# Splitting the first weights of two experts whole instead of in halves, inside a fused attention and two mixture-of-experts layers

## The chip, the cores and the metric

The kernel runs on one core of a Trainium2 chip. The metric is the time of one execution on the device in microseconds (us), the median of several runs; less is better. Engines are named as the profile names them: PE is TensorE, DVE is VectorE, ACT is ScalarE, POOL is GpSimd, SP is the engine that issues most DMAs.

## What is computed

Three layers follow each other, all on float32 inputs: a linear attention with a root-mean-square norm, a mixture of experts in which every token goes through all four experts, and a soft mixture with eight experts of four slots. The second layer is the long one:

```python
N, D, E, F = (2304, 512, 4, 1024)
p = domain_probs / (domain_probs.sum(-1, keepdims=True) + 1e-09)
out = np.zeros((N, D), dtype=np.float32)
for e in range(E):
    h = np.maximum(x @ w1[e], 0.0)
    out += p[:, e:e + 1] * (h @ w2[e])
```

The output must agree with a float32 reference, so a float16 product alone would be too coarse.

## The kernel before

**Products.** Each float32 operand is scaled and split into two float16 pieces, a high one (the rounded value) and a low one (what is left). A product is then three float16 matmuls: high by high, high by low, low by high. On top of this, each large product is a 2 by 2 block product done with seven block products instead of eight (Winograd's form). So each expert's w1, which arrives as four raw pages of 128 by 1024 (blocks 0 to 3), is turned into seven operands, B11, B21, B22 and T1 to T4, of which the T are differences of raw blocks (T1 = block 1 - block 0, T2 = block 3 - T1, T3 = block 3 - block 1, T4 = block 2 - T2). SBUF is managed as 47 pages of 128 by 1024 floats.

**Splitting.** The function split (lines 612 to 619) makes one operand's pieces: the high piece by an ACT instruction (line 615), the low piece by a DVE instruction (line 617). Each takes 512 columns of an operand in this kernel (the method put, line 666), apart from expert 0, whose w1 is split 1024 columns at a time with the methods hi and lo (lines 670 and 673) at the start of the program. The differences are made by make (line 643, a DVE instruction of 1024 columns at line 652). The same split is used for w2 (line 712) and for differences of w2 blocks (prep_t2, line 722, whose subtractions are line 735).

**Main list.** The 18 tiles of 128 tokens are taken in chunks: chunks 0 and 1 first (four tiles each), then the rest. The program builds one list of 542 steps, each about 1.3 us of PE work. A step of mm1 is one half of one of the seven block products with w1 (12 matmuls of 256 columns, line 926); a step of mm2 multiplies with w2 (line 989, the plain form, 6 matmuls of 512 columns into one bank for each tile of tokens, read out by DVE at line 1001), and a step of mm2_fast does a block product of the second layer (12 matmuls of 256 columns, line 1029). For experts 1 and 2 the order of the steps is mm1 of chunk 0, mm1 of chunk 1, mm2 of chunk 0 (16 steps), mm2_fast of chunk 1 (14 steps). For expert 1 these are steps 60 to 73, 74 to 87, 88 to 103 and 104 to 117; for expert 2 the same from 118 to 175.

**mm2_fast and its banks.** The seven block products come in the order 1, 7, 6, 4, 5, 2, 3 (ORDER3), each as two steps (two pairs of tiles, j = 0 and 1). Products 1, 6, 5, 3 accumulate in one bank ("x"), 7 and 4 in a second, 2 in a third. After each product DVE reads both halves of the bank and adds them into the output (line 1051, two instructions). Product 6 writes into the bank of product 1, so it waits until DVE has read product 1 out of it. Product 1 takes the bank that the second token tile of mm2 has left, product 7 that of the third.

**Evictions of mm1 for chunk 1.** They run in fast_h: DVE adds product 2 (line 864), 7 (line 868) and 3 (line 872) to what ACT has copied, ACT and DVE split the sums (lines 834, 836 and 841, 845), and a queue of further work (todo: lines 879, 883, 849) is taken off one item a step.

**Background work.** Preparations run beside the main list as chains: a chain is a list of small steps that is spread over a range of main steps by a credit, with a weight per main step that depends on the phase.

```python
credit += wt[0] * (len(steps) - credit) / max(sum(wt), 1e-3)
n = min(int(credit + 1e-6), max(1, -(-len(steps) // len(wt))))
```

Engines execute what is issued to them in program order, so where a chain's step falls decides what DVE and ACT do before what. The weights of expert e (2 or 3) are prepared by one chain over the steps of expert e - 1: prep_w1 and then prep_w2. prep_w1 is 10 steps that find the scale (the four w_size are ACT instructions, line 538), then 15 steps that split 14 halves; step n of these issues the low piece of half n - 1 and the high piece of half n. The weights of the phases are 0.5, 0.1, 0.5 and 1.0, so few steps fall into mm1 of chunk 1. At the same time a second chain, prep_t2 of expert e - 1, runs.

Of the kernel before, what the change touches and what calls it, by code (L numbers as in the profile page):

```python
# [33 lines left out]
B11, B21, B22, T1, T2, T3, T4 = range(7)  # L34
# [13 lines left out]
def attn_moe_softmoe_kernel(ctx: ExitStack, tc: tile.TileContext, qT, k, v, g, dp, w1, w2, phi, m1, m2a, m2b, out):  # L48
# [482 lines left out]
    def w_size(e, nm, b):  # L531

        m = wmx.get((e, nm))
        if m is None:
            m = wmx[e, nm] = small.tile([128, 4], F32, tag=f"mx{nm}", name=f"mx_{nm}_{e}")
        src = need((nm, 0, e, b)).ap
        junk = work.tile([128, 1024], BF16, tag="junk", name=f"junk{e}_{b}")
        nc.scalar.activation(junk, src, AF.Square if nm == "w1" else AF.Abs, accum_out=m[:, b:b + 1])  # L538
# [24 lines left out]
    def scale_steps(e, nm):  # L563

        return [lambda: w_scale_a(e, nm), lambda: None, lambda: None, lambda: None, lambda: pe(lambda: w_spread(e, nm)),
                lambda: w_scale_b(e, nm)]
# [45 lines left out]
    def split(dst, src, s, part):  # L612

        if part == 0:
            nc.scalar.activation(dst[:, 0], src, AF.Copy, scale=s)  # L615
        else:
            nc.vector.scalar_tensor_tensor(  # L617
                out=dst[:, 1], in0=src, scalar=s, in1=dst[:, 0], op0=ALU.mult, op1=ALU.subtract
            )

    class PrepW1:
# [44 lines left out]
        def put(self, op, i, part):  # L666
            dst = self.page(op).rearrange("p (s k n) -> p s k n", s=2, k=2)
            split(dst[:, :, i], self.src(op).f32(2)[:, i], wpw[self.k[1], "w1"][1], part)
# [11 lines left out]
    def prep_w1(g_, e, eng):  # L680
        w = PrepW1(g_, e, eng)
        st = []
        if g_ == 0:
            st += [lambda b=b: w_size(e, "w1", b) for b in range(4)]
            st += scale_steps(e, "w1")

        then = {
            B11: lambda: w.make(T2),
            T2: lambda: w.make(T4),
            T1: lambda: w.t1.release(),  # L690
            T4: lambda: (w.drop(0), w.drop(2)),
            T3: lambda: w.drop(1),
            B22: lambda: w.drop(3),
        }
        seq = [(op, i) for op in (B11, B21, T2, T1, T3, B22, T4) for i in range(2)]

        def step(n):
            if n == 0:
                w.make(T1)
            if n == 2:  # L700
                w.make(T3)
            if n > 0:
                op, i = seq[n - 1]
                w.put(op, i, 1)
                if i == 1 and op in then:
                    then[op]()
            if n < len(seq):
                w.put(*seq[n], 0)

        return st + [lambda n=n: step(n) for n in range(len(seq) + 1)]  # L710

    def w2_split(e, b, key, i, part):
        pgs = w2p.setdefault((0 if key == b or e > 0 else 1, e), {})
# [262 lines left out]
    def mm2(wk, c, t, u, kk, first, bank=ps_o):  # L976
        if t // 2 not in acc:
            acc[t // 2] = Page(first)
        o = (t - CH[c][0]) * 128
        if u == 0 and kk == 0:  # L980
            yps[t] = bank(f"y{wk[0]}_{wk[1]}_{t}")
        ps = yps[t]
        h = h_view(c, u, kk)
        w = w2_page(wk, 2 * kk + u).f16().rearrange("p (s f n) -> p s f n", s=2, f=2)
        for fp in range(2):
            hh, hl = (h[:, s, fp, o:o + 128] for s in range(2))
            wh, wl = (w[:, s, fp] for s in range(2))
            for i, (a, b) in enumerate(((hh, wh), (hh, wl), (hl, wh))):
                nc.tensor.matmul(  # L989
                    ps, a, b, start=(u + kk + fp + i == 0), stop=(u == 1 and kk == 1 and fp == 1 and i == 2)  # L990
                )
        work_off(1)
        if u == 0 or kk == 0:
            return
        del yps[t]
        x = acc_f32(t)
        pc = pcs[wk[1]][:, t:t + 1]
        if first:
            nc.vector.tensor_scalar(out=x, in0=ps, scalar1=pc, scalar2=None, op0=ALU.mult)
        else:  # L1000
            nc.vector.scalar_tensor_tensor(out=x, in0=ps, scalar=pc, in1=x, op0=ALU.mult, op1=ALU.add)
# [284 lines left out]
    for gi, cs in enumerate(GR):  # L1286
        for ei, e in enumerate(EXP[gi]):
# [5 lines left out]
            seq = [(i, c) for c in cs for i in (1, 2)]  # L1293
            if gi == 0 and e in SOON:
                seq = [(i, c) for i in (1, 2) for c in cs]
            if gi == 1:
                seq = LASTSEQ if ei == E - 1 else FASTSEQ
            runs.append((e, [(gi, i, c) for i, c in seq]))
    for e, seq in runs:
        if True:  # L1300
            for n, (gi, which, c) in enumerate(seq):
# [12 lines left out]
                if which == 1:  # L1314
                    if not turns:
                        own, other = ps_x, ps_o
                    st = [lambda wk=wk, c=c, u=u, P=P, fast=fast, bank=own: mm1(wk, c, u, P, fast, bank)
                          for P in ORDER for u in range(2)]
# [8 lines left out]
                elif fast:  # L1327
                    st = [lambda wk=wk, c=c, P=P, j=j, bank=own, ei=ei, apart=other if last and done else None:
                          mm2_fast(wk, c, P, j, bank, ei == 0, apart)
                          for P in ORDER3 for j in range(len(ch) // 2)]  # L1330
# [3 lines left out]
                else:  # L1334

                    tu = [(ch[0], 0), (ch[1], 0), (ch[0], 1), (ch[1], 1)] + [(t, u) for t in ch[2:] for u in range(2)]
                    st = [
                        lambda wk=wk, c=c, t=t, u=u, kk=kk, ei=ei, b=(own, other, other, own)[t % 4] if soon else ps_o:
                        mm2(wk, c, t, u, kk, ei == 0, b)
                        for t, u in tu for kk in range(2)  # L1340
                    ]
# [63 lines left out]
    for e in range(1, E):  # L1405
        chain(m["mm2", 0, 0, 0] + 12 if e == 1 else m["mm1", 0, e - 1, 0], m["end", 0, e - 1, 1] - 1,
              prep_w1(0, e, V) + prep_w2(0, e), 12 if e == 1 else 6,
              W1 if e == 1 else by_phase(e - 1, 0.5, 0.1, 0.5, 1.0))
# [60 lines left out]
    with tc.manual_schedule():  # L1469
# [13 lines left out]
        w = PrepW1(0, 0, nc.vector)  # L1483
# [392 lines left out]
```

## Time and profile before

| | |
|---|---|
| median of 3 runs | 812.72 us (812.07 to 816.3) |
| profiled execution, its own time | 812.28 us |
| its span, first to last instruction | 810.5 us |
| PE busy | 794.8 us, 98% |
| DVE busy | 579.3 us, 71% |
| ACT busy | 404.4 us, 50% |
| DMA | 126.03 MB, mean 155 GB/s |

All parts below come from the one profiled execution. Busy times of PE come from matmuls that overlap each other, and their ends are modelled, so a busy PE can still lose a little; where it waits, the timeline shows a gap with the instruction that ended it. [...]

### The profile page before, as it was taken

The numbers are of one execution on the slowest core, as the hardware profiler recorded it, in microseconds if no ns is written. First come the engines' busy times: TensorE is split into PE (matmuls) and PEld (weight loads), VectorE is DVE, ScalarE is ACT, GpSimd is POOL, SyncE is SP. The second block draws the span as 40 slices with busy tenths as digits, with TensorE's granted clock in tenths as the row PEclk, the third lists the DMA queues.
The fourth block names the chain that finished last, engine by engine and source line by source line (L and its number), as shares of the span: only waits on it lengthen the run. The fifth ranks groups of instructions, "written<-read, shape, count | busy, mean of one in ns | idle before, by whom it ended". The sixth has DMA issues, their size and how long they took to land.

```text
span 810.5 us, 17979 instructions
## 1 busy us (share of the span) xinstructions
PE 794.8 (98%) x7630; PEld 651.2 (80%) x7630; DVE 579.3 (71%) x1145; ACT 404.4 (50%) x791; POOL 5.9 (1%) x14
## 2 busy tenths in 40 slices
PE   8999999999999999999999999999999999999996
PEld 8876768668857867888988888998889889887544
DVE  6997968986998467789779547874578548676403
ACT  5876766566656244684656446231544137322203
POOL 0000000000000000000000000000000000000000
PEclk9999999999999999999999999999999999999998
DMA  9961532376417700200015750045004132669897
GB/s 359 404 256 46 192 153 79 130 260 235 155 62 261 251 1 10 71 2 1 1 53 186 283 183 1 19 165 206 4 1 169 66 131 79 242 214 339 311 398 239
DMA packets 40753, 126.03 MB, mean 155 GB/s; under 512 B 4066, under 2 KB 11106, under 8 KB 40674
## 3 DMA queue, kind: packets, MB, share of 16 engines
q1 hardware_dynamic: 40016, 124.57, 42.3%
q8 instruction: 59, 0.97, 0.5%
q10 hardware_dynamic: 658, 0.33, 0.1%
q14 instruction: 20, 0.16, 0.1%
HBM read 96.57 MB, written 28.31 MB: 154 GB/s over the span
## 4 chain that ended last, share of the span: by engine, by line
PE 90%; DVE 7%; ACT 1%; issue 1%; DVEq 0%; POOL 0%; POOLq 0%; ACTq 0%
PE p L926 38%; PE m L1029 26%; PE y L989 13%; PE s L1725 2%; PE so L1755 2%; PE o L340 2%; PE keep L265 2%; PE kv L285 1%; DVE pages L617 1%; PE x2T L1068 1%; PE xT L405 1%; PE lg L1097 1%; DVE pages L1051 1%; DVE pages L845 1%; PE f L1788 1%
## 5 line engine op out<-in xcount | busy, mean ns | idle before, releaser
L926 PE MATMUL p<-pages 128*128 128x256 f16 (+1 forms) x3360 | 339.0, 262 | 0.5 <-ACT cT L1233 0.5
L926 PEld LDWEIGHTS <-pages 128*128 128x128 f16 x3360 | 299.8, 98 | 33.3 <-issue 2.0
L1029 PE MATMUL m<-pages 128*128 128x256 f16 x2184 | 244.7, 273 | 2.8 <-DVE pages L1051 1.6
L1029 PEld LDWEIGHTS <-pages 128*128 128x128 f16 x2184 | 213.0, 98 | 29.8 <-issue 3.7
L1051 DVE SCALAR_TENSOR_TENSOR pages<-m,pc,pages 128x256 f32<-128x256 f32 x162 | 72.3, 480 | 59.3 <-PE m L1029 58.7
L989 PE MATMUL y<-pages 128*128 128x512 f16 x480 | 106.1, 379 | 0.3 <-DVE pages L943 0.3
L989 PEld LDWEIGHTS <-pages 128*128 128x128 f16 x480 | 46.9, 98 | 54.1 <-DVE pages L943 0.8
L617 DVE SCALAR_TENSOR_TENSOR pages<-pages,s_w 128x512 f16<-128x512 f32 (+1 forms) x113 | 84.7, 780 | 3.3 <-ACT pages L615 3.0
L836 ACT CAST pages<-t 128x512 f16<-128x512 f32 (+1 forms) x90 | 49.9, 562 | 72.6 <-DVE t L879 36.7
L615 ACT ACTIVATE pages<-pages,s_w 128x512 f16<-128x512 f32 (+1 forms) x113 | 79.1, 742 | 12.9 <-DVE s_w L591 9.7
L845 DVE TENSOR_TENSOR pages<-t,pages 128x512 f16<-128x512 f32 (+1 forms) x90 | 54.2, 614 | 3.4 <-ACT pages L836 2.3
L834 ACT ACTIVATE pages<-pages 128x512 f16<-128x512 f32 (+1 forms) x60 | 34.4, 574 | 40.2 <-DVE pages L868 20.2
L836 ACT CAST pages<-pages 128x512 f16<-128x512 f32 (+1 forms) x30 | 16.8, 562 | 44.8 <-DVE t L883 44.8
L956 DVE TENSOR_TENSOR t<-p,t 128x512 f32<-128x512 f32 x30 | 20.5, 690 | 24.7 <-PE p L926 24.5
L868 DVE TENSOR_TENSOR pages<-p,pages 128x512 f32<-128x512 f32 (+1 forms) x30 | 18.6, 619 | 27.1 <-PE p L926 25.9
L841 DVE SCALAR_TENSOR_TENSOR pages<-pages 128x512 f16<-128x512 f32 (+1 forms) x60 | 35.5, 613 | 0.7 <-ACT pages L834 0.2
L538 ACT ACTIVATE junk<-pages 128x1024 bf16<-128x1024 f32 x32 | 33.8, 1055 | 3.0 <-DMA pages<-in_w 2.5
L864 DVE TENSOR_TENSOR t<-p,t 128x512 f32<-128x512 f32 (+1 forms) x30 | 18.4, 618 | 23.3 <-PE p L926 22.2
L858 ACT COPY t<-p 128x512 f32<-128x512 f32 (+1 forms) x30 | 15.7, 528 | 34.4 <-PE p L926 34.4
L942 ACT ACTIVATE pages<-t 128x512 f16<-128x512 f32 x30 | 18.9, 630 | 23.0 <-DVE t L956 22.8
L951 ACT COPY t<-p 128x512 f32<-128x512 f32 x30 | 17.1, 582 | 22.4 <-PE p L926 22.4
L834 ACT ACTIVATE pages<-t 128x512 f16<-128x512 f32 (+1 forms) x30 | 17.2, 574 | 21.6 <-DVE t L864 21.6
(187 smaller groups left out, 709.6 us busy)
## 6 DMA issues: line engine op xcount, KB each, us to landing
pages<-in_w SPq DMA_DIRECT2D x48, 512.0 KB, 6.2
o<-pages SPq DMA_DIRECT2D x33, 512.0 KB, 6.9
pages<-o SPq DMA_DIRECT2D x33, 512.0 KB, 6.3
pages<-in_m SPq DMA_DIRECT2D x32, 512.0 KB, 5.2
pages<-in_m2a SPq DMA_DIRECT2D x16, 512.0 KB, 5.1
pages<-in_m2b SPq DMA_DIRECT2D x16, 512.0 KB, 10.2
o_t<-pages SPq DMA_DIRECT2D x12, 512.0 KB, 2.6
pages<-o_t SPq DMA_DIRECT2D x12, 512.0 KB, 5.5
```

The source lines that it names most:

```text
L538: nc.scalar.activation(junk, src, AF.Square if nm == "w1" else AF.Abs, accum_out=m[:, b:b + 1])
L615: nc.scalar.activation(dst[:, 0], src, AF.Copy, scale=s)
L617: nc.vector.scalar_tensor_tensor(out=dst[:, 1], in0=src, scalar=s, in1=dst[:, 0], op0=ALU.mult, op1=ALU.subtract)
L834: nc.scalar.activation(dst, sh(src), AF.Relu)
L836: nc.scalar.copy(dst, sh(src))
L841: nc.vector.scalar_tensor_tensor(out=h[:, 1], in0=sh(src), scalar=0.0, in1=h[:, 0], op0=ALU.max, op1=ALU.subtract)
L845: nc.vector.tensor_tensor(out=h[:, 1], in0=sh(src), in1=h[:, 0], op=ALU.subtract)
L926: nc.tensor.matmul(ps[:, fp * n:fp * n + n], l, r, start=(fp + i == 0 and P in first), stop=(fp == 1 and i == len(mms) - 1 and P in end), ...
L956: nc.vector.tensor_tensor(out=t, in0=ps, in1=t, op=ALU.add)
L989: nc.tensor.matmul(ps, a, b, start=(u + kk + fp + i == 0), stop=(u == 1 and kk == 1 and fp == 1 and i == 2))
L1029: nc.tensor.matmul(ps, l, r, start=(i == 0 and (j == 0 or each) and P in (1, 2, 7)), stop=(i == len(mms) - 1 and (j == nh - 1 or each) and ...
L1051: nc.vector.scalar_tensor_tensor(out=x, in0=src, scalar=pc, in1=x, op0=ALU.mult, op1=ALU.add)
```

## The change

For experts 2 and 3 prep_w1 splits each operand whole: one ACT instruction of 1024 columns for the high piece and one DVE instruction of 1024 columns for the low one, by hi and lo. The 15 splitting steps of the chain become 8, and ahead of each of the 8 a step without work is put, so that the chain has 26 steps instead of 25 before prep_w2. The scaling steps, the differences, expert 0 and 1, and prep_w2 stay as they are.

```diff
-            T1: lambda: w.t1.release(),
+            T1: lambda: None if wide else w.t1.release(),
...
-        seq = [(op, i) for op in (B11, B21, T2, T1, T3, B22, T4) for i in range(2)]
+        wide = e > 1
+        seq = [(op, i) for op in (B11, B21, T2, T1, T3, B22, T4) for i in range(1 if wide else 2)]
+
+        def put(op, i, part):
+            (w.lo if part else w.hi)(op) if wide else w.put(op, i, part)
 
         def step(n):
             if n == 0:
                 w.make(T1)
-            if n == 2:
+            if n == (1 if wide else 2):
                 w.make(T3)
             if n > 0:
                 op, i = seq[n - 1]
-                w.put(op, i, 1)
-                if i == 1 and op in then:
+                put(op, i, 1)
+                if i == (not wide) and op in then:
                     then[op]()
             if n < len(seq):
-                w.put(*seq[n], 0)
-
-        return st + [lambda n=n: step(n) for n in range(len(seq) + 1)]
+                put(*seq[n], 0)
+
+        st += [lambda n=n: step(n) for n in range(len(seq) + 1)]
+        if wide:
+            for k in range(len(st) - 1, 9, -1):
+                st.insert(k, lambda: None)
+        return st
```

Lines below the diff stand 8 higher in the changed kernel (868 becomes 876, 1051 becomes 1059). In the rows that follow, s_w_2 with a number is the scale of expert 2's w1 (so line 617 with it is a low piece of the operands that the change touches), s_w_1_1264 that of expert 1's w2. Expert 3's rows stand in the same order one expert later.

For expert 2 the splitting steps fell on main steps 73, 76, 82, 89, 90, 92 to 96, 98 to 101 and 105; now the 8 steps with work fall on 75, 89, 91, 93, 96, 98, 101 and 105. The step that issues the differences T3 and T2 moves from 82, in mm1 of chunk 1, to 89, in mm2 of chunk 0.

First place, DVE in mm1 of chunk 1, between the eviction of product 2 and that of product 7. Before:

```order
L841 SCALAR_TENSOR_TENSOR pages<-t_0_1_1_1_1610,pages 128x512
L652 TENSOR_TENSOR pages<-pages 128x1024
L617 SCALAR_TENSOR_TENSOR pages<-pages,s_w_2_1540 128x512
L652 TENSOR_TENSOR pages<-pages 128x1024
L735 TENSOR_TENSOR pages<-pages 128x2x256
L868 TENSOR_TENSOR pages<-p_0_1_1_0_1578,pages 128x512
```

In the changed kernel, the same place:

```order
L849 SCALAR_TENSOR_TENSOR pages<-t_0_1_1_0_1589,pages 128x512
L849 SCALAR_TENSOR_TENSOR pages<-t_0_1_1_1_1610,pages 128x512
L743 TENSOR_TENSOR pages<-pages 128x2x256
L876 TENSOR_TENSOR pages<-p_0_1_1_0_1576,pages 128x512
L743 TENSOR_TENSOR pages<-pages 128x2x256
```

Two differences (T3 and T2) and the low half between them no longer stand here; the low half of main step 76, somewhat earlier, is gone too.

Second place, DVE at the start of mm2 of chunk 0, from the last work on product 4 of mm1. Before:

```order
L879 SCALAR_TENSOR_TENSOR t_0_1_1_1_1610<-t_0_1_1_1_1610,pages 128x512
L617 SCALAR_TENSOR_TENSOR pages<-pages,s_w_2_1540 128x512
L845 TENSOR_TENSOR pages<-t_0_1_1_0_1591,pages 128x512
L617 SCALAR_TENSOR_TENSOR pages<-pages,s_w_2_1540 128x512
L617 SCALAR_TENSOR_TENSOR pages<-pages,s_w_1_1264 128x512
L845 TENSOR_TENSOR pages<-t_0_1_1_1_1610,pages 128x512
```

In the changed kernel:

```order
L887 SCALAR_TENSOR_TENSOR t_0_1_1_1_1610<-t_0_1_1_1_1610,pages 128x512
L652 TENSOR_TENSOR pages<-pages 128x1024
L617 SCALAR_TENSOR_TENSOR pages<-pages,s_w_2_1524 128x1024
L652 TENSOR_TENSOR pages<-pages 128x1024
L853 TENSOR_TENSOR pages<-t_0_1_1_0_1589,pages 128x512
L617 SCALAR_TENSOR_TENSOR pages<-pages,s_w_1_1264 128x512
L853 TENSOR_TENSOR pages<-t_0_1_1_1_1610,pages 128x512
```

The two differences, with the whole low piece of B11 between them, now stand together behind the last instruction that belongs to mm1.

Third place, DVE at the end of mm2 of chunk 0 and the start of mm2_fast of chunk 1 (y_1_2 and y_1_3 are the third and fourth token tile, the m behind them is product 1). Before:

```order
L849 SCALAR_TENSOR_TENSOR t_0_1_1_0_1591<-pages,t_0_1_1_0_1591 128x512
L1001 SCALAR_TENSOR_TENSOR pages<-y_1_2_1903,pc_1269,pages 128x512
L617 SCALAR_TENSOR_TENSOR pages<-pages,s_w_2_1540 128x512
L849 SCALAR_TENSOR_TENSOR t_0_1_1_1_1610<-pages,t_0_1_1_1_1610 128x512
L617 SCALAR_TENSOR_TENSOR pages<-pages,s_w_2_1540 128x512
L845 TENSOR_TENSOR pages<-t_0_1_1_0_1591,pages 128x512
L845 TENSOR_TENSOR pages<-t_0_1_1_1_1610,pages 128x512
L1001 SCALAR_TENSOR_TENSOR pages<-y_1_3_1943,pc_1269,pages 128x512
L617 SCALAR_TENSOR_TENSOR pages<-pages,s_w_2_1540 128x512
L1051 SCALAR_TENSOR_TENSOR pages<-m_0_1_1_0_1977,pc_1269,pages 128x256 x2
```

In the changed kernel:

```order
L857 SCALAR_TENSOR_TENSOR t_0_1_1_0_1589<-pages,t_0_1_1_0_1589 128x512
L1009 SCALAR_TENSOR_TENSOR pages<-y_1_2_1892,pc_1269,pages 128x512
L857 SCALAR_TENSOR_TENSOR t_0_1_1_1_1610<-pages,t_0_1_1_1_1610 128x512
L617 SCALAR_TENSOR_TENSOR pages<-pages,s_w_2_1524 128x1024
L853 TENSOR_TENSOR pages<-t_0_1_1_0_1589,pages 128x512
L853 TENSOR_TENSOR pages<-t_0_1_1_1_1610,pages 128x512
L1009 SCALAR_TENSOR_TENSOR pages<-y_1_3_1929,pc_1269,pages 128x512
L617 SCALAR_TENSOR_TENSOR pages<-pages,s_w_2_1524 128x1024
L1059 SCALAR_TENSOR_TENSOR pages<-m_0_1_1_0_1963,pc_1269,pages 128x256 x2
```

The two readings of product 1 stand behind a whole low piece instead of a half. Between the second place's first row and these readings DVE had 12 halves and one difference (T4) of expert 2; it now has 7 whole pieces and three differences. Everything else in between is the same.

## Rows read from the trace of the kernel before

**Rows 1.** The page: the granted TensorE clock in 40 slices.
```profile
PEclk9999999999999999999999999999999999999998
```
**Rows 2.** The chain that ended last, in order of time: start us, us, what.
```profile
151.72 20.72 PE y L989 x96
172.44 9.17 PE m L1029 x84
```
**Rows 3.** Windows: busy us and count of PE, PEld, DVE, ACT, POOL, clock, DMA.
```profile
141.50:153.40 11.90, 11.90 (x103) 9.88 (x102) 11.75 (x19) 6.15 (x11) 0.00 (x0) 1.00 0.47 158
153.40:172.30 18.90, 18.90 (x90) 8.54 (x88) 18.82 (x30) 12.07 (x21) 0.00 (x0) 1.00 0.41 138
```
**Rows 4.** Timeline of DVE in mm1 of chunk 1, expert 1: start us, us, instruction, count.
```profile
141.55 1.22 DVE L652 TENSOR_TENSOR pages<-pages 128x1024 f32<-128x1024 f32 x1
...
143.46 1.22 DVE L652 TENSOR_TENSOR pages<-pages 128x1024 f32<-128x1024 f32 x1
144.61 0.68 DVE L735 TENSOR_TENSOR pages<-pages 128x512 f32<-128x512 f32 x1
145.28 0.69 DVE L868 TENSOR_TENSOR pages<-p,pages 128x512 f32<-128x512 f32 x1
```
**Rows 5.** Timeline of PE there: the last 204 matmuls of mm1 for expert 1.
```profile
129.29 22.43 PE L926 MATMUL p<-pages 128*128 128x256 f16 x204
```
**Rows 6.** Timeline of DVE in mm2 of chunk 0, expert 1.
```profile
153.40 0.75 DVE L617 SCALAR_TENSOR_TENSOR pages<-pages,s_w 128x512 f16<-128x512 f32 x1
154.06 0.68 DVE L845 TENSOR_TENSOR pages<-t,pages 128x512 f16<-128x512 f32 x1
...
160.03 1.23 DVE L652 TENSOR_TENSOR pages<-pages 128x1024 f32<-128x1024 f32 x1
161.18 0.68 DVE L883 SCALAR_TENSOR_TENSOR t<-pages,t 128x512 f32<-128x512 f32 x1
...
171.34 0.75 DVE L1001 SCALAR_TENSOR_TENSOR pages<-y,pc,pages 128x512 f32<-128x512 f32 x1
```
**Rows 7.** Timeline of DVE at the start of mm2_fast: the readings of products 1 and 7.
```profile
176.45 0.87 DVE L1051 SCALAR_TENSOR_TENSOR pages<-m,pc,pages 128x256 f32<-128x256 f32 x2
177.72 0.88 DVE L1051 SCALAR_TENSOR_TENSOR pages<-m,pc,pages 128x256 f32<-128x256 f32 x2 [0.40 <-PE m L1029]
```
**Rows 8.** Timeline of PE there: the first 84 matmuls of mm2_fast.
```profile
172.28 9.33 PE L1029 MATMUL m<-pages 128*128 128x256 f16 x84
```
**Rows 9.** Timeline of DVE and of ACT: whole pieces of expert 0, 1024 columns each.
```profile
14.03 2.48 DVE L617 SCALAR_TENSOR_TENSOR pages<-pages,s_w 128x1024 f16<-128x1024 f32 x2
...
12.84 3.23 ACT L615 ACTIVATE pages<-pages,s_w 128x1024 f16<-128x1024 f32 x3 [1.94 <-DVE s_w L589]
```
**Rows 10.** Timeline of DVE and PE in a later mm2_fast, where PE waits.
```profile
382.61 0.87 DVE L1051 SCALAR_TENSOR_TENSOR pages<-m,pc,pages 128x256 f32<-128x256 f32 x2
...
383.54 0.92 PE L1029 MATMUL m<-pages 128*128 128x256 f16 x7 [1.58 <-DVE pages L1051]
```
**Rows 11.** Timeline of DVE one expert later: product 1 is read.
```profile
252.64 0.88 DVE L1051 SCALAR_TENSOR_TENSOR pages<-m,pc,pages 128x256 f32<-128x256 f32 x2
```
**Rows 12.** Timeline of PE one expert later: the first matmuls of mm2_fast.
```profile
248.47 9.33 PE L1029 MATMUL m<-pages 128*128 128x256 f16 x84
```
**Rows 13.** Timeline of ACT around the end of mm2 of chunk 0.
```profile
161.95 0.62 ACT L836 CAST pages<-pages 128x512 f16<-128x512 f32 x1 [3.51 <-DVE t L883]
...
174.53 1.04 ACT L538 ACTIVATE junk<-pages 128x1024 bf16<-128x1024 f32 x1
```
**Rows 14.** Timeline of SP: loads of expert 2's last w2 blocks, among others.
```profile
166.66 3.27 SPq L164 DMA_DIRECT2D pages<-in_w  x2
```
**Rows 15.** Windows near the wait of rows 10, in the loading phase, and at the end.
```profile
380.00:384.00 4.00, 2.42 (x23) 2.02 (x22) 3.97 (x11) 1.91 (x4) 0.00 (x0) 1.00 0.00 0
...
760.00:780.00 20.00, 19.27 (x180) 8.32 (x182) 5.08 (x19) 2.20 (x9) 1.87 (x2) 1.00 1.00 386
...
805.00:806.00 1.00, 0.00 (x0) 0.00 (x0) 0.00 (x0) 0.00 (x0) 0.00 (x0) 0.74 1.02 272
```

## Prediction

> **What bounds the kernel now.** I read the granted clock first, then the chain that ended last, then windows over the stretch that the change touches, then the timelines of the engines there. The clock is full in every slice but the last [rows 1]. The chain in order of time is PE alone from expert 1's first mm1 to the end of expert 2's mm2_fast; in the stretch where expert 2's weights are split it goes from mm2 of chunk 0 straight into mm2_fast [rows 2]. PE is busy for all of 141.5 to 172.3 us [rows 3]. So there is no idle time of PE for this change to give back. But DVE is busy for 11.75 of 11.90 us and then for 18.82 of 18.90 us in the same windows [rows 3]. It works through a backlog, and what counts is whether each reading that PE waits for still comes in time.
>
> The tightest one is the reading of product 1 in mm2_fast. PE's 84 matmuls from 172.28 us take 9.33 us, of which the last one's own 0.27 us is no spacing, so they start 0.109 us apart [rows 8]. A block product is 24 of them, 2.62 us. Product 7 begins at 172.28 + 2.62 = 174.90 us and product 6, which writes into product 1's bank, at 172.28 + 5.24 = 177.52 us. DVE has read product 1 out at 176.45 + 0.87 = 177.32 us [rows 7]. In a later mm2_fast PE did wait for such a pair of readings: they ended at 382.61 + 0.87 = 383.48 us, PE went on at 383.54 us, 0.06 us later [rows 10]. So product 6 could have started at 177.38 us, and the margin is **0.14 us**. One expert later it is the same: 248.47 + 5.24 = 253.71 us [rows 12] against 252.64 + 0.88 + 0.06 = 253.58 us [rows 11]. And the reading was late not for want of data: DVE went to it straight from the split of the last half, 1.5 us after product 1 was complete.
>
> **The change part by part**, for expert 2; expert 3 has the same rows 76.2 us later.
>
> *Wide pieces on DVE.* A half costs DVE 154.06 - 153.40 = 0.66 us from its start to the next one's [rows 6]. Two whole pieces took 2.48 us, and one alone 1.28, so a whole one costs 1.20 us [rows 9]. Seven whole ones for 14 halves: 14 x 0.66 - 7 x 1.20 = 0.84 us less work. [...] The row shows 0.12 us for each pair and is used here.
>
> *Wide pieces on ACT.* They only shorten its work, and it has room: it stood still for 3.51 us until DVE had made its input [rows 13]. The whole high piece of T4 now comes after a cast that waits for the later DVE, so the four size measurements of w2, which begin at 174.53 us [rows 13], start some 1.7 us later. DVE needs their result only after product 1 and 7 are read. Nothing on the path; nothing is taken for it.
>
> *The moved step.* Main step 82 issued T3, a low half and T2; main step 76 a low half. All of it now comes in or after main step 89, behind the last DVE work of mm1. What DVE does instead in mm1: it would come to the w2 subtraction (line 735) at 141.55 us instead of 144.61 [rows 4], and then to product 7's eviction. But product 7's first half is complete only with the 144th of the 204 matmuls from 129.29 us, 143 spacings of 0.109 us and 0.27 us for the last: 145.18 us [rows 5]. In the kernel before, DVE read it at 145.28 us [rows 4], so it cannot do so earlier. DVE will stand idle there for about 3.6 us, and from 145.28 us to 153.40 us its rows are unchanged. The work that filled this hole, 2 x 1.15 + 2 x 0.66 = 3.62 us, is added to a stretch in which it has no idle time. A difference costs 161.18 - 160.03 = 1.15 us [rows 6].
>
> *The sum in that stretch.* From 153.40 us to the readings of product 1, DVE had 12 halves and one difference of expert 2, 12 x 0.66 + 1.15 = 9.07 us. It now has 7 whole pieces and 3 differences, 7 x 1.20 + 3 x 1.15 = 11.85 us. That is 2.78 us more; the 0.08 us that it idled in 153.4 to 172.3 us [rows 3] go off: **2.70 us**. Checked the other way: 3.62 moved in less 0.84 saved is 2.78. Product 1 is then read at 177.32 + 2.70 = 180.02 us, product 6 starts at 180.08 instead of 177.52 us: PE stands still for **2.56 us**.
>
> *What else waits there.* Product 7 needs the bank of the third token tile, read out at 171.34 + 0.75 = 172.09 us [rows 6]. Up to that point DVE had 9 halves and one difference and now has 5 whole pieces and three, 2.36 us more: 174.45 us, 0.45 us before product 7 begins. It holds, barely. Product 4 follows product 6 at 182.70 us and needs product 7's readings, done at about 180.9. Behind PE's wait all its later work shifts as one.
>
> *The empty steps.* They issue nothing. They only set where the 8 real steps fall.
>
> *Loads.* SP issues the same DMAs in the same order. The two w2 loads at 166.66 us [rows 14] now wait for DVE's whole pieces of T1 and T3, about 3 us later; they are needed by size measurements that start at or after 176 us and land, as others there, some 8 us after issue at most, the last one in use near 180 us. Nothing on the path. POOL's instructions are the same and none is passed.
>
> *Total.* Two experts at 2.56 us are 5.1 us. Against the profiled execution's own time of 812.28 us that makes **817.4 us**, 0.63% more. The median of the runs, 812.72 us, is 0.4 us higher than that execution, which is within the spread of the runs.
>
> *Unknown sizes.* That product 6 waits for both readings of the pair and not for the first alone is read from one wait [rows 10]; for the first alone the hold would be 0.40 us shorter, 2.16 us each, so 816.6 us. If the other small waits of DVE are taken up too, 2.0 us each, 816.3. If a whole piece saved nothing over two halves, 0.84 us more each: 3.4 us, 819.1 us. I take 2.56 because both rows it rests on, the pair's end and the whole piece's 1.20 us, are of the very instructions.
>
> **The rivals.**
>
> *Not slower: DVE has less to do, and PE is not held.* DVE is saturated [rows 3], and 0.84 us less for it would bring the readings forward, not back. [...] Then PE still waits for nothing, and as it has no idle time there, the time stays at 812.3 us. It decides at product 1's readings: if they move back by less than 0.14 us, there is no loss. For it speaks the busy share; against it that DVE reads product 7 at 145.28 us, 0.1 us after it is complete, so that the engine is not ahead but in step, and work taken away before that point is time lost [rows 4, 5].
>
> *The loss is taken up at the end.* From 760 to 780 us the DMA engines are busy all the time [rows 15]; if loading the last layer's weights, not PE, set the end, a part of the 5.1 us would vanish, 814.8 us with half of it. Against it: the loads are issued when PE frees pages, so they are shifted too.
>
> [...]
>
> That the change does not do what it says can be left out: the order of the rows shows the pieces whole and the step moved.
>
> **How the numbers follow.** The forecast, 816.3 to 819.1 us, has 0.74; no hold 0.11; a part taken up 0.10; the clock 0.05. The range that leaves out the clock, the no-hold case and the lower third of the partial one, together 0.19, is 814.0 to 819.1 us. About 0.5%, 4.06 us, is what a measurement can tell from no change; that is 816.8 us against the median. Slower by more than that: 0.64 of the forecast's 0.74 and the clock's 0.05, 0.69. Within it: the forecast's other 0.10, the partial case and 0.08 of the no-hold case, 0.28. Faster: no row shows where 4 us could come from; 0.03 out of the no-hold case.
>
> **What would show it.** Right: PE has a gap of about 2.5 us in the third block product of mm2_fast for experts 1 and 2, ended by line 1059, and none elsewhere in the stretch; DVE idles some 3.6 us before product 7's eviction in mm1 of chunk 1; its whole pieces take 1.28 us. Wrong: no such gap, product 1's readings ending before 177.5 us, a gap at product 7 too, or a clock below 1.00 behind the gap.

## The result and the profile after

The changed kernel takes 819.23 us, the median of 5 executions (818.87 to 819.94), against 812.5 us (812.07 to 816.3) before; the ratio is 1.0079, 95% interval 1.0068 to 1.0090. Measured once more, in a later series, it took 818.88 us against 812.87, ratio 1.0063 (1.0045 to 1.0082). It is slower by more than 0.5%, as forecast; the time lies 1.8 us above the forecast of 817.4 us and 0.1 us above the upper end of the range. The profiled execution took 819.33 us with a span of 817.5 us, 7.0 us longer than before.

The page first: the granted TensorE clock in 40 slices, in tenths of full speed, and the shares of the chain that ended last. In the kernel before the chain was 90% PE and 7% DVE.

```profile
PEclk9999999999999999999999999999999999999998
...
PE 81%; DVE 13%; ACT 3%; issue 2%; DVEq 0%; POOL 0%; ACTq 0%; POOLq 0%
```

The slices hide what follows: each is 20 us wide. The windows of the stretch, which answer to [rows 3], show DVE's busy time (third pair) in 141.5 to 153.4 us down from 11.75 to 8.24 us, and unchanged, so full, behind it:

```profile
141.50:153.40 11.90, 11.90 (x105) 9.99 (x103) 8.24 (x14) 5.46 (x10) 0.00 (x0) 1.00 0.41 127
153.40:172.30 18.90, 18.90 (x89) 8.58 (x88) 18.83 (x24) 10.91 (x15) 0.00 (x0) 1.00 0.31 114
```

The timeline of DVE, expert 1, beside [rows 4, 6, 7]:

```profile
141.34 0.68 DVE L743 TENSOR_TENSOR pages<-pages 128x512 f32<-128x512 f32 x1
145.56 0.69 DVE L876 TENSOR_TENSOR pages<-p,pages 128x512 f32<-128x512 f32 x1 [3.54 <-PE p L934]
...
171.50 1.28 DVE L617 SCALAR_TENSOR_TENSOR pages<-pages,s_w 128x1024 f16<-128x1024 f32 x1
172.70 0.68 DVE L853 TENSOR_TENSOR pages<-t,pages 128x512 f16<-128x512 f32 x1
...
173.90 0.74 DVE L1009 SCALAR_TENSOR_TENSOR pages<-y,pc,pages 128x512 f32<-128x512 f32 x1
...
178.22 1.28 DVE L617 SCALAR_TENSOR_TENSOR pages<-pages,s_w 128x1024 f16<-128x1024 f32 x1
179.41 1.65 DVE L1059 SCALAR_TENSOR_TENSOR pages<-m,pc,pages 128x256 f32<-128x256 f32 x4
```

There is the hole of 3.54 us ahead of product 7's eviction, a whole piece that takes 172.70 - 171.50 = 1.20 us from start to start, and the readings of product 1, which now begin at 179.41 us (176.45 before). And the timeline of PE in both mm2_fast, beside [rows 8, 12]:

```profile
172.56 5.40 PE L1037 MATMUL m<-pages 128*128 128x256 f16 x48
180.34 5.76 PE L1037 MATMUL m<-pages 128*128 128x256 f16 x36 [2.37 <-ACT junk L538]
185.93 0.39 PE L558 MATMUL ar_w<-dg_w,ones 128*128 128x128 f32 x2
186.15 9.33 PE L1037 MATMUL m<-pages 128*128 128x256 f16 x84
...
252.95 5.40 PE L1037 MATMUL m<-pages 128*128 128x256 f16 x48
260.72 4.09 PE L1037 MATMUL m<-pages 128*128 128x256 f16 x36 [2.37 <-ACT junk L538]
264.65 0.39 PE L558 MATMUL ar_w<-dg_w,ones 128*128 128x128 f32 x2
264.87 9.33 PE L1037 MATMUL m<-pages 128*128 128x256 f16 x84
```

PE stops after 48 matmuls, two block products, and goes on when the pair of readings is done: 179.41 + 0.87 = 180.28 us, 0.06 us before 180.34. The row names an ACT instruction instead, because one ended at about the same moment, at 180.35 us: the third of the four size measurements, in the timeline of ACT

```profile
180.16 0.19 ACT L538 ACTIVATION_READ_ACCUMULATOR junk<-pages 128x1 f32 x1
```

The experiments below show that it is DVE. The 36 matmuls behind the first gap take 5.76 us, those behind the second 4.09. The windows show why (the last three columns are the granted clock as a share of full speed, DMA share and GB/s):

```profile
178.00:180.40 2.40, 0.06 (x1) 0.06 (x1) 2.40 (x5) 2.32 (x5) 0.00 (x0) 1.00 1.04 422
180.40:181.40 1.00, 1.00 (x10) 0.90 (x10) 0.67 (x2) 1.00 (x2) 0.00 (x0) 1.00 0.99 406
181.40:182.40 1.00, 1.00 (x7) 0.72 (x6) 0.44 (x2) 0.13 (x2) 0.00 (x0) 0.52 1.03 401
182.40:184.40 2.00, 2.00 (x12) 1.34 (x10) 0.00 (x0) 0.00 (x0) 0.00 (x0) 0.50 0.72 287
...
185.40:186.40 1.00, 1.00 (x12) 0.92 (x10) 0.15 (x2) 0.00 (x0) 0.00 (x0) 1.00 0.03 12
258.30:260.80 2.50, 0.13 (x2) 0.08 (x1) 2.50 (x5) 2.41 (x6) 0.00 (x0) 1.00 1.02 392
260.80:263.40 2.60, 2.60 (x25) 2.32 (x25) 1.09 (x4) 1.11 (x2) 0.00 (x0) 1.00 1.03 421
```

About 1 us after PE went on, the clock fell to 0.50 for some 3.4 us; behind the second gap, 2.37 us like the first, it stayed at 1.00.

The chain, in order of time (start us, us, what), was PE alone in this stretch [rows 2]. It now goes from PE to DVE at the end of the hole, when product 7 is complete, and comes back to PE only after the gap. The pieces left out are mostly DVE's; from 175.80 us on they are ACT's, because the chain follows the releaser that the row above names:

```profile
140.00 5.47 PE p L934 x50
145.52 0.04 issue
145.56 0.06 DVE pages L876
...
180.35 1.67 PE m L1037 x12
```

**Where the time went**, by the starts of PE's rows: mm2_fast of expert 1 begins at 172.56 instead of 172.28 us, 0.28 us later, all of it from the first 12 us of the program, where the 54 matmuls that begin at 3.7 us took 8.04 us instead of 7.76 (6.90 to 8.40 in the executions of the experiments). Product 6 begins 180.34 - 172.56 - 5.24 = 2.54 us late. From there to the second half of mm2_fast it takes 186.15 - 180.34 = 5.81 us where 9.39 - 5.24 = 4.15 us stood before: there mm2_fast began at 172.28 us and its second half at 181.67, 9.39 us later, in the timeline of PE of the kernel before

```profile
181.67 9.33 PE L1029 MATMUL m<-pages 128*128 128x256 f16 x84
```

So the fall of the clock to 0.50 costs 1.66 us. In expert 2 the gap is 260.72 - 252.95 - 5.24 = 2.53 us. The sum is 0.28 + 2.54 + 1.66 + 2.53 = 7.01 us, the whole difference of the spans.

### The profile page after: what moved, and what is told of

Read it like the earlier page. It is cut to its first block, busy times and chain, and to the rows that moved or that the text cites. A ratio compares the mean times of both kernels' runs of the same rounds, so it can differ in the third digit from the quotient of the medians.

```text
span 817.5 us, 17954 instructions
## 1 busy us (share of the span) xinstructions
PE 797.0 (97%) x7630; PEld 652.1 (80%) x7630; DVE 577.7 (71%) x1131; ACT 401.4 (49%) x777; POOL 5.9 (1%) x14
## 4 chain that ended last, share of the span: by engine, by line
PE 81%; DVE 13%; ACT 3%; issue 2%; DVEq 0%; POOL 0%; ACTq 0%; POOLq 0%
PE p L934 36%; PE m L1037 25%; PE y L997 7%; DVE pages L617 3%; PE s L1733 2%; PE so L1763 2%; PE o L340 2%; DVE pages L853 2%; PE keep L265 2%; PE kv L285 1%; DVE pages L849 1%; PE x2T L1076 1%; PE xT L405 1%; PE lg L1105 1%; DVE pages L1059 1%
## 5 line engine op out<-in xcount | busy, mean ns | idle before, releaser
L617 DVE SCALAR_TENSOR_TENSOR pages<-pages,s_w 128x512 f16<-128x512 f32 (+1 forms) x99 | 82.5, 858 | 3.2 <-ACT pages L615 3.0
L615 ACT ACTIVATE pages<-pages,s_w 128x512 f16<-128x512 f32 (+1 forms) x99 | 75.8, 805 | 17.6 <-DVE s_w L591 12.4
```

Source lines behind the costliest of these rows:

```text
L617: nc.vector.scalar_tensor_tensor(out=dst[:, 1], in0=src, scalar=s, in1=dst[:, 0], op0=ALU.mult, op1=ALU.subtract)
```

## The experiments

The theory: the moved step costs the time, because DVE, which cannot fill its hole, has 2.7 us more to do between product 7's eviction and the readings of product 1. Rivals: the longer instructions themselves hold PE; PE waits for something else, the size measurements on ACT or loads.

**1. Whole pieces, the step kept at its old place.** One empty step fewer, so that T3 and T2 are issued on main step 82 again. The edit, against the changed kernel:

```diff
-            for k in range(len(st) - 1, 9, -1):
+            for k in range(len(st) - 1, 10, -1):
```

> Whole pieces as in the change, but with an empty step between two splitting steps and none ahead of the first, so that T3 and T2 stay in mm1 of chunk 1, on main step 82. Theory (the moved step is the cost, the whole piece a small gain): from the start of mm2 to the readings of product 1 DVE has 6 whole pieces and 1 difference of the next expert where the kernel before had 12 halves and 1, 0.7 us less; the readings of product 1 end about 0.7 us earlier than before, at some 176.6 us of the kernel before's clock, no gap of PE in mm2_fast of experts 1 and 2, clock 1.00 throughout, time that of the kernel before, 812.5 us within 0.5. Rival (whole pieces themselves hold PE, by blocking the readings behind longer instructions): gaps of some 2.4 us stay and the time is 817 us or more.

Measured: 812.95 us against 812.46, ratio 1.0006 (0.9997 to 1.0015). The timeline of PE and DVE in mm2_fast of expert 1 and the one of expert 2:

```profile
172.47 9.33 PE L1037 MATMUL m<-pages 128*128 128x256 f16 x84
...
248.66 9.33 PE L1037 MATMUL m<-pages 128*128 128x256 f16 x84
...
176.09 0.87 DVE L1059 SCALAR_TENSOR_TENSOR pages<-m,pc,pages 128x256 f32<-128x256 f32 x2
177.91 0.88 DVE L1059 SCALAR_TENSOR_TENSOR pages<-m,pc,pages 128x256 f32<-128x256 f32 x2 [0.96 <-PE m L1037]
```

84 matmuls run through without a gap in both, in 9.33 us as in [rows 8, 12]. The readings begin at 176.09 us in a program that started 0.19 us late, 0.55 us earlier than before (0.7 expected), so the whole pieces did save DVE time; DVE then waits 0.96 us for PE (0.40 before), and PE, which never waited, gains nothing. Width is not the cost.

**2. The moved step, with halves.** The 8 steps and the empty ones of the change, each operand as two halves:

```diff
-            (w.lo if part else w.hi)(op) if wide else w.put(op, i, part)
+            if wide:
+                w.put(op, 0, part)
+                w.put(op, 1, part)
...
+            else:
+                w.put(op, i, part)
```

> The 8 splitting steps and the empty steps of the change, but each operand in two halves inside its step: the moved step alone, without the wider instructions. Theory: DVE has 7 x 0.12 us more than in the change before it reads product 1, so PE's gap at product 6 is 2.37 + 0.84 = 3.2 us for each of the two experts, and with the lower clock after the first of them as in the change the time is 819.2 + 1.7 = 820.9 us; without a fall of the clock 819.2. Rival (the width is the cost): no gap, 812.5 us.

Measured: 822.17 us (820.9 expected), ratio 1.0119 (1.0105 to 1.0133). The timeline of PE in both mm2_fast and of DVE before the readings:

```profile
173.09 5.57 PE L1043 MATMUL m<-pages 128*128 128x256 f16 x48
181.78 5.76 PE L1043 MATMUL m<-pages 128*128 128x256 f16 x36 [3.12 <-DVE pages L1065]
...
263.07 4.09 PE L1043 MATMUL m<-pages 128*128 128x256 f16 x36 [3.12 <-DVE pages L1065]
...
179.53 1.41 DVE L617 SCALAR_TENSOR_TENSOR pages<-pages,s_w 128x512 f16<-128x512 f32 x2
180.85 1.66 DVE L1065 SCALAR_TENSOR_TENSOR pages<-m,pc,pages 128x256 f32<-128x256 f32 x4
```

Product 6 is late by 181.78 - 173.09 - 5.24 = 3.45 us, 0.91 us more than with whole pieces (0.84 expected); 0.17 of it, 5.57 - 5.40, is a small wait at product 7, where the change left 0.54 us of margin. This execution also started 0.81 us late and shows the same lower clock behind the first gap alone, 0.50 in 183.0 to 186.0 us and 5.76 us for 36 matmuls. So the place of the step makes the loss and the whole pieces make it smaller.

**3. One expert at a time.** `wide = e == 3` and `wide = e == 2` in place of `wide = e > 1`; the first was measured twice.

> The change for expert 3 alone; expert 2 is split as in the kernel before. Theory: one gap of 2.4 us, in mm2_fast of expert 2, none in that of expert 1; 812.5 + 2.5 = 815.0 us if the clock stays full behind it, as behind the second gap of the change. Rival on the clock (the first long gap of a run lowers it, whichever it is): 816.7 us and a granted clock near 0.5 for some 3.5 us behind the gap.

> The change for expert 2 alone; expert 3 is split as in the kernel before. Theory: one gap of 2.4 us in mm2_fast of expert 1 and the lower clock behind it as in the change: 812.5 + 2.5 + 1.7 = 816.7 us. If the fall of the clock needs something else than this gap, 815.0 us. With the run for expert 3 alone the two differences to the kernel before should add up to the 6.7 us of the change.

> The change for expert 3 alone once more, since the profiled execution had lost 2.1 us before the first of these gaps and the runs lay at 814.8 and at 817. If the loss at the start is chance, the executions without it and without a fall of the clock lie at 815.0 us, those with a fall at 816.7. If it belongs to this kernel, the profile shows the same 1.8 us gap at the first products of the attention part again.

Expert 3 alone took 817.21 us the first time, ratio 1.0055 (1.0042 to 1.0068), and 815.1 us the second, 1.0036 (1.0023 to 1.0050); expert 2 alone 816.59 us, 1.0049 (1.0035 to 1.0063). Each has one gap, at product 6 of the mm2_fast before that expert, late by 2.54 us (258.34 - 250.56 - 5.24 in the first run of expert 3). The times are of two kinds: for expert 3, executions with a mean clock of 0.997 took 814.5 to 815.1 us (4 of 10), those with 0.995 took 816.9 to 818.0 us (6). The five of expert 2 alone, 814.84 to 818.55 us at 0.993 to 0.997, do not sort so cleanly. The profiled execution of the first run had lost 2.09 us at the start of the program, by a later load (a gap of 1.84 us) and a lower clock there (0.88 in 14 to 20 us, 0.90 in 20 to 30 us), and shows full clock behind its gap, 1.00 in 258 to 261 us. That of the second shows the fall behind expert 3's own gap, in the timeline of PE and in a window:

```profile
256.83 5.76 PE L1037 MATMUL m<-pages 128*128 128x256 f16 x36 [2.35 <-DVE pages L1059]
262.64 9.33 PE L1037 MATMUL m<-pages 128*128 128x256 f16 x84
...
257.80:260.80 3.00, 3.00 (x17) 2.12 (x16) 0.45 (x2) 0.22 (x2) 0.00 (x0) 0.52 0.84 339
```

So the gaps add up, 2.54 us each in the traces. The medians add up only with the second run of expert 3 alone: 2.51 and 4.13 us above the kernel before are 6.64, where 6.7 was expected; the first, 4.75 us above, gives 8.88, since the start (2.09 us lost there) and the mean clock (0.993 to 0.997) differ between executions. The fall of the clock does not belong to the first gap, to expert 1 or to the changed kernel, and the same gap of the same kernel had it in one execution and not in another. It is also the same gap that is put down here to DVE's line 1059 and in the changed kernel to ACT.

**4. One piece behind the readings.** The last splitting step, the whole low piece of T4, is issued one main step later, behind the readings of product 1:

```diff
+            hooks.setdefault(m["mm2", 0, e - 1, 1] + 2, []).append(st[-1])
+            st[-1] = lambda: None
```

> The change, but the last splitting step of experts 2 and 3 (the whole low piece of T4) stands behind the readings of product 1 instead of ahead of them; the step with T3 and T2 stays on 89. Theory (what DVE does ahead of the readings of product 1 is the whole cost): these end 1.20 us earlier than in the change, PE's gap at product 6 is 2.37 - 1.20 = 1.2 us for both experts, and the time is 812.5 + 2 x 1.34 = 815.2 us with the clock full, or 816.8 us if it falls once as in the change. Rival (product 6 waits for something else, the size measurements on ACT that the trace of the change names, or the loads): the gap stays 2.4 us, 817.5 to 819.2 us.

Measured: 815.16 us (814.86 to 815.52 in 6 executions), ratio 1.0029 (1.0017 to 1.0040). The timeline of PE and DVE:

```profile
178.86 4.09 PE L1039 MATMUL m<-pages 128*128 128x256 f16 x36 [1.15 <-DVE pages L1061]
...
256.37 4.09 PE L1039 MATMUL m<-pages 128*128 128x256 f16 x36 [1.16 <-DVE pages L1061]
...
177.95 0.86 DVE L1061 SCALAR_TENSOR_TENSOR pages<-m,pc,pages 128x256 f32<-128x256 f32 x2
178.73 1.27 DVE L617 SCALAR_TENSOR_TENSOR pages<-pages,s_w 128x1024 f16<-128x1024 f32 x1
```

The piece of 1.20 us taken from ahead of the readings takes 1.22 us from the gap (2.37 to 1.15), twice, and no execution shows a lower clock. The size measurements of the next expert stand where they stood: less the start of the program, the third ends at the same time as in the change, here at 180.08 us, 1.22 us after product 6 has begun. The rival with ACT falls. Of the loads, the two of expert 2's last w2 blocks are issued when they were, those behind them 1.4 us earlier (173.92 - 172.31 against 175.61 - 172.56 us behind the start of mm2_fast); no row names a load as what PE waits for.

**5. Two pieces behind the readings.** The low piece of B22 goes behind the readings of product 1, that of T4 behind those of product 7; the step with T3 and T2 stays on 89 and the hole in mm1 stays:

```diff
+            for k, n in ((-3, 2), (-1, 4)):
+                hooks.setdefault(m["mm2", 0, e - 1, 1] + n, []).append(st[k])
+                st[k] = lambda: None
```

> The change, but the last two splitting steps stand behind the readings: the low piece of B22 (with the high one of T4) behind those of product 1, the low one of T4 behind those of product 7. The step with T3 and T2 stays on 89, and DVE still idles 3.5 us in mm1 of chunk 1. Theory: the readings of product 1 end 2.4 us earlier than in the change, 0.14 us too late for each expert; no gap that the trace would list, clock full, 812.5 + 0.3 = 812.8 us. Rival (the hole in mm1 or the moved step costs in itself, or product 4 or 6 waits in place of it): 814 us or more.

Measured: 813.77 us, ratio 1.0014 (1.0005 to 1.0023), a miss by 1 us and nearer the rival's 814 us than the forecast. The timeline of PE and DVE:

```profile
172.99 9.62 PE L1040 MATMUL m<-pages 128*128 128x256 f16 x84
182.51 0.49 PE L558 MATMUL ar_w<-dg_w,ones 128*128 128x128 f32 x2
182.83 7.37 PE L1040 MATMUL m<-pages 128*128 128x256 f16 x66
...
175.58 1.46 DVE L856 TENSOR_TENSOR pages<-t,pages 128x512 f16<-128x512 f32 x2
```

PE loses 182.83 - 172.99 - 9.39 = 0.45 us for each expert, not 0.14: 9.62 - 9.33 = 0.29 us at product 6, half of it because two DVE instructions now take 1.46 us (1.29 in the change), by the author's estimate with a short wait for their input that the whole piece had hidden; the rest at the small matmuls of the scale. Another 0.71 us of this execution is at the start of the program. So the rival is right in so far as product 6 still waits a little. What counts for the theory holds: with the step on 89, the hole unfilled and all pieces whole, the gap is all but gone once less stands ahead of the readings.

**6. The same remedy where the kernel before waits.** To experiment 1 was added, for the mm2_fast of [rows 10], that two low pieces of a later chunk are not taken off the queue ahead of the readings of product 5:

```diff
-        work_off(1, c, op)
+        work_off(0 if (wk, c, P) == ((0, 3), 1, 5) else 1, c, op)
```

> As the first of these runs (whole pieces, the step with T3 and T2 on main step 82), and in the one mm2_fast in which PE waited 1.58 us in the kernel before, two low pieces of a later chunk (128 x 512, 0.60 us each) are taken off the queue one product later, so that they stand behind the readings of the fifth block product. By the same theory the gap shrinks by 1.2 us to 0.4 us, and the time to 811.3 us, 0.15% below the kernel before. Rival (the two pieces come due elsewhere and hold PE there): 812.5 us with the gap moved.

Measured: 812.83 us, ratio 1.0000 (0.9992 to 1.0009). The timeline of PE, first of this run, from the gap of [rows 10] to the mm1 of the last, smaller chunk:

```profile
382.50 2.78 PE L1037 MATMUL m<-pages 128*128 128x256 f16 x24 [0.62 <-DVE pages L1059]
...
432.62 2.29 PE L934 MATMUL p<-pages 128*128 128x128 f16 x36 [0.21 <-ACT t L866]
435.24 4.44 PE L934 MATMUL p<-pages 128*128 128x128 f16 x72 [0.33 <-DVE t L872]
439.84 0.83 PE L934 MATMUL p<-pages 128*128 128x128 f16 x12 [0.16 <-DVE pages L876]
440.50 0.71 PE L1037 MATMUL m<-pages 128*128 128x256 f16 x5
```

and of experiment 1 in that mm1:

```profile
432.08 8.87 PE L934 MATMUL p<-pages 128*128 128x128 f16 x156 [0.46 <-ACT cT L1241]
440.79 0.93 PE L1037 MATMUL m<-pages 128*128 128x256 f16 x7
```

The gap shrank by 0.96 us, from 1.58 to 0.62, and PE was 1.23 us ahead of experiment 1 (0.26 of it from the start of the program) when it came to the small chunk, whose evictions PE waits for there. Behind it 440.79 - 440.50 = 0.29 us was left: the gain was given back in the next place where PE waits for evictions, as the rival had it; whether the two moved pieces or other work of DVE held those evictions was not separated. No version was faster than the kernel before.

This profiled execution took 813.70 us, 1.2 us more than that of experiment 1, although it was still 0.29 us ahead at 763 us. The window of the last layer, which answers to the second line of [rows 15], shows why:

```profile
760.00:780.00 20.00, 19.28 (x159) 7.69 (x161) 4.33 (x19) 1.91 (x7) 1.84 (x2) 0.91 0.94 351
```

The mean clock is 0.91 over these 20 us, which cost 1.50 us by the starts of PE's rows (763.02 to 789.71 us against 763.31 to 788.50 in experiment 1), though no gap of PE from 735 us to the start of those rows is longer than 0.36 us. The kernel before, with a gap of 0.36 us at 763.12 us, and experiment 1 have a clock of 1.00 in the same window.

**7. The changed kernel again**, for the clock.

> The changed kernel once more, for the clock behind its two gaps: without a fall it should take 812.5 + 2 x 2.54 = 817.6 us, with one 819.2, with two 820.9. If exactly one of two equal gaps lowers the clock in every execution, all lie near 819.2 us; if each gap does so by itself about every second time, as the runs with one gap alone would have it, times near 817.6 and 820.9 appear too, and the profiled execution may show the fall behind another gap than the first.

Measured: 818.88 us. In both series together 8 of 11 executions have a mean clock of 0.995 and took 818.7 to 819.9 us; three have 0.997 and took 817.7 to 818.9. The mean clock does not say where the fall was; the profile does, for one execution of each series. The profiled execution again shows the fall behind the first gap (0.62 in 180.4 to 183.0 us, 0.76 in 183 to 186) and a full clock behind the second (1.00 in 261 to 266 us). No execution lies near 820.9 us.

## Why the prediction was right and where it was not

- *The bound and the place*: right. PE waits at the third block product of mm2_fast for experts 1 and 2, and nowhere else in the stretch; DVE's queue ahead of the readings is the cause (experiments 1, 2, 4 and 5).
- *Wide pieces on DVE, 1.20 us each*: right, 1.20 us. Experiment 2 puts the saving of seven at 0.91 us, 0.84 was taken.
- *The moved step*: right. The hole was forecast as 3.6 us and is 3.54. One reading was incomplete: the w2 subtraction was to begin at 141.55 us and begins at 141.34 - 0.28 = 141.06, since main step 76's half, which the prediction does count in its 3.62 us, no longer stands ahead of it either.
- *The sum*: 2.56 us for each expert forecast, 2.54 and 2.53 measured. The two readings were to end at 180.02 us; less the 0.28 us of the start they end at 180.00.
- *Product 7*: forecast to hold by 0.45 us. Its bank was read out at 173.90 + 0.74 = 174.64 us and it began at 172.56 + 2.62 = 175.18, 0.54 us to spare. Experiment 2 shows how near that was.
- *ACT, loads, empty steps at nothing*: right. The size measurements begin 2.0 us later than before where 1.7 was forecast (176.85 - 0.28 against 174.53 us), and nothing on PE's path waits for that; the four terms above add up to the whole difference of the spans.
- *The rival without a hold* fell with the trace, *the loss taken up at the end* too: PE is 7.01 us late at 264.87 us and the span is 7.0 us longer.
- *The clock falls*: this step failed. It was given a chance of 0.05, an estimate of the author's that no run shows, and left out of the range. Behind the one gap of 1.58 us of the kernel before the clock stayed full [rows 10, 15], but a gap of that size says nothing of one of 2.4 us: in both profiled executions of the changed kernel the clock fell, behind one of the two gaps only, and cost 1.66 us in the first and 1.67 in the second. A clock below 1.00 behind the gap was also one of the prediction's own signs of being wrong. With this term and the 0.28 us of the start the sum is 812.28 + 5.07 + 1.66 + 0.28 = 819.29 us, and the profiled execution took 819.33.

## What to carry to other kernels

Work that was taken from a full engine's queue is a saving only if it does not leave a hole in front of data that come at a fixed time; what moves behind such a point adds to the queue in full, here 3.6 us against 0.84 us saved. So count what stands between the last point at which the engine waits for data and the reading for which another engine waits, and compare it with that reading's margin, here 0.14 us. Where a spreading rule places steps by their number, look at what a changed number moves before looking at what the instructions cost, and price a stop of PE with its clock, from a gap at least as long, as a cost that comes in some executions and not in others, here 1.66 or 1.67 us behind 4 of 7 gaps of 2.35 to 2.37 us.

## What the runs showed of the hardware

Behind gaps of PE of 2.35 to 2.37 us the profiled executions show a fall of the clock in 4 of 7 cases (the change 1 of 2, its repetition 1 of 2, expert 2 alone 1 of 1, expert 3 alone 1 of 2), behind 3.12 us in 1 of 2, behind the 1.15 and 1.16 us of experiment 4 in none, and behind the 1.58 us of [rows 10] in none. Each of these falls cost 1.66 or 1.67 us and began within about 1 us after PE had gone on, not in the gap; the lowest windows within them have 0.50 (the change, 182.4 to 184.4 us, and experiment 2). A single gap of that length is not needed: in experiment 6 the clock fell in the last layer, to a mean of 0.91 in 760 to 780 us, with no gap over 0.36 us near, and in the first run of expert 3 alone it fell behind the 1.84 us gap at the start, to a mean of 0.88 in 14 to 20 us. The kernel before, too, has executions with a mean clock of 0.995 or less, in the series of experiments 4 to 6 four of 22, at 813.7 to 813.9 us; where their clock fell was not profiled. What decides between two equal gaps stays open; in no execution that was profiled did it fall behind both.

A gap's releaser is an inference: the same wait was put down to ACT's line 538 in one execution and to DVE's line 1059 in the next, because both ended within 0.1 us of each other, in the change at 180.28 and 180.35 us. The run that moved one DVE instruction (experiment 4) told them apart: the gap shrank by that instruction's time while the measurements of ACT stayed.

Not tried: a bank of its own for product 6, whose sums are accumulated on product 1's, and other work of DVE to fill the hole in mm1.
